# Twelve output tiles take x*Dskip from GpSimd instead of TensorE

## The chip, the cores and the metric

The kernel runs on one core of a Trainium2 chip. The metric is the device time of one execution in microseconds (us), as the median of several runs. Beside the runs there is one profiled execution, from which all views of the profile come. The engines are TensorE (PE, with its weight loads PEld), VectorE (DVE), ScalarE (ACT), GpSimd (POOL) and SyncE (SP, which here only issues DMAs). An ending q (SPq, ACTq, POOLq) means the queue on which an engine issues DMAs.

## The reference, cut to what matters

```python
x = A_x                                          # [1, 2048, 512] bf16
g = sigmoid((x * gate_w).sum(-1, keepdims=True))
a = _A_ref(x, ...)     # h[t] = Lam_bar * h[t-1] + x[t] @ B_bar ; y = 2 Re(h @ C^T) + x * Dskip
b = _B_ref(x, ...)     # linear attention, 32 heads of 16; the features are softmax(pq) and softmax(-pq)
return g * a + (1 - g) * b
```

The change concerns the term `x * Dskip` of `a`, which enters the output as `g * x * Dskip`.

## The kernel before

The 2048 rows of x are read as 16 tiles of 128 rows, with the columns transposed (`xT`, SP's DMA transposes, L229). Rows go to tiles by their residue modulo 8: tile `ti` holds the residue `r = ti // 2` of one half `a = ti % 2` of the sequence. So the scan over time becomes, for each residue, products with precomputed powers (steps g, h, z), and only residue 7 is scanned (L641).

The kernel is cut into **steps** with short names. Each is a Python generator; each `yield` ends a piece of it. A string `ORDER` (L24 to L53) lists the pieces of all steps in one order, and the loop at L804 runs down it. PE, DVE, ACT and SP take their instructions exactly in this order; POOL isn't among the engines whose order is fixed by hand (L154), but takes them as the program emits them. `@` behind a name gives the PSUM banks for what the piece allocates, `:D` puts a copy on DVE instead of ACT, `:A` puts a store on ACT's queue instead of SP's. An engine that waits in one piece holds up everything behind it in its own list. Tokens without an engine's work, such as END, only change which memory is in use.

The steps that matter here, by number n of the tile in output order (n = 0 to 15; `ti = order[n]`):

- **k, v, q** (L477 to L496): keys, values and queries, four matmuls of 512 columns each, and a copy out of PSUM.
- **X, N, E, S** for groups 1 to 3 of the query features, four tiles at a time (group 1 is tiles 4 to 7, group 2 is 8 to 11, group 3 is 12 to 15): X and N (L516, L524) take maximum and minimum by trees on DVE (L511) and subtract (L521, L527); E (L530) takes four exponentials on ACT (L138, a helper's line); S (L536) sums by a tree on DVE, takes logarithm and exponential on ACT, multiplies on DVE (L559) and then issues four DMA transposes (L563) on SP, which write `phT`. The names xA, nA, eA, sA stand for group 0, and lower-case x, n, e, s for the keys.
- **G** (L677): the gate g in four small pieces, the last a reciprocal on DVE (L684).
- **y** (L711): `py = h @ C`, two pieces of four matmuls (L717), and a third piece that adds x*Dskip: for each of four column blocks, `xT` times the diagonal matrix `Dd` (L722), into the same PSUM bank.
- **o** (L725): the attention's numerator and denominator from `phT` and `KVm` into `pn` (L736), a logarithm and a copy `nu` for each half, an exponential `rd` that takes in (1-g)/g, the product `on` on DVE (L744), and its transpose `oT`, by a DMA on SP (L758) or, for n = 12 to 15, on PE (L753).
- **t** (L761): `py += oT @ Wo` on PE (L765), then the tile is scaled by g on ACT (L769) or DVE (L771) as it leaves PSUM, then the store (L773).

So the last piece of a tile's PSUM sum is t's, and the scaling by g follows it:

```python
ot = pools["op"][1].tile([P, D], BF16, name="ot", bufs=14)
if sel["eng"] == "act":
    nc.scalar.mul(out=ot[:], in_=py[:], mul=G[:, ti:ti + 1])
else:
    VS(out=ot[:], in0=py[:], scalar1=G[:, ti:ti + 1], scalar2=None, op0=ALU.mult)
```

The memory of the query stage is taken at END (L696), when the pools of the key stage are given back.

Of the kernel before, what the change touches and what calls it, by code (L numbers as in the profile page):

```python
# [10 lines left out]
ALU = mybir.AluOpType  # L11
# [9 lines left out]
P = 128  # L21
# [8 lines left out]
a0@71 a0 x2 s1 x2 s1 v5 g00@4 g00 g60@0 n2 x3 s1 g20@3 g60 s1 g10@2 g10 n3 e2 g30@6 g40@5 g10 s1 a1 x3 g20 n3 a1 x3 n3  # L30
x3 g41@4 n3 C3 e2 e2 e2 x3 g30 g40 g30 k15@0 k15 n3 e3 s2 x4 s2 x4 g01@2 g01 e3 e3 s2 g50@3 g11@5 g50 s2 s2 s2 n4 x4
n4 Q3 n4 s2 g50 g21@6 e3 s3 v8@0 g31@2 g11 Q2 g11 n4 g70@3 Q1 s3 C7 g21 g70 v9@5 g70 g70 z0 z0 g31 g31 Q0 w1@6 C0 a2
a2 a2 w0@3 s3 z0 v11@2 v9 g61@5 g41 R4 z0 w1 v8 z0 z0 g61 s3 w2@4 s3 s3 a2 x4 z0 z0 g51@6 g51 x4 w2 C2 s3 w3@0 g51 v11
n4 R5 w3 g71@5 g71 g71 g71 z1 z1 g02@4 g02 g42@6 a3 a3 z0 z0 g42 w0 e4 e4 z1 z1 z1 g62@2 g12@0 q1@5 C1 h50@4 C5 J1 e4
# [10 lines left out]
S1 y1 E2 E2 E2 E2 y9@6 G N3 y5 y5 y3@4 y2 X3 X3 N3 t1 G t1 N3 S1 N3 S2 y9 y9 S2 S2 S1 S1 S2 y3 y3 t3 y0 t0 t0 t2 t2
y6@7 X3 t2:A o4@2 o4 o4@5 o4 o4 y6 y6 t3 X3 o4 X3 o4 S2 S2 t3 o5@1 o5 o5@2 o5 o5 y13@5 y13 o5 N3 o6@4 S2 o6 o6@1 o6 o6
y12@2 o5 y7@4 y7 y12 o6 o6 t4 y7 S2 S2 t4:D S2 E3 E3 E3 E3 S2 o7@1 o7 t5 t5 S3 o7@0 o7 S3 o7 t6 S3 o7 S2 o7 y8@1 o8@3
t6 o8 o8@0 o8 o8 S3 S3 y12 t0:A y11@7 o8 o8 o9@3 o9:D o9@0 o9:D S3 y8 y8 o9 o9 S3 S3 o9 o10@3 y11 o10 o10@0 y11 o10
o10 S3 y14@3 S3 y14 t7 t7:D t8 y14 t8 y15@0 o11@4 S3 o11 o11@1 t9 o12@4 o11:D o11 S3 o10 o10 o12 o12@1 o12 o12 t9:D
# [19 lines left out]
def kernel(  # L69
# [26 lines left out]
    NR = 8  # L96
# [614 lines left out]
    def st_y(n):  # L711
# [49 lines left out]
    def st_t(n):  # L761
# [5 lines left out]
        ot = pools["op"][1].tile([P, D], BF16, name="ot", bufs=14)  # L767
        if sel["eng"] == "act":
            nc.scalar.mul(out=ot[:], in_=py[:], mul=G[:, ti:ti + 1])  # L769
        else:  # L770
# [8 lines left out]
          "M": st_M(), "D": st_D(), "L": st_L(), "G": st_G(), "Y": st_Y(), "END": st_END(), "NR": st_N(0), "NI": st_N(1), "O": st_O()}  # L779
# [35 lines left out]
    for key in ("op", "fq", "eq", "sq"):  # L815
        pools[key][0].__exit__(None, None, None)
# [31 lines left out]
```

## Time and profile before

| | us |
|---|---|
| three runs: median (lowest to highest) | 155.84 (155.54 to 156.19) |
| profiled execution, first to last instruction | 153.2 |
| PE busy in it | 146.2 |
| DVE busy in it | 132.4 |
| ACT busy in it | 129.2 |
| POOL busy in it | 15.8 |

The profiled execution's own time is its span, 153.2 us; the runs' time is taken around the whole execution and also holds what lies before the first and after the last instruction. A busy PE is not PE at its peak: matmuls are pipelined, and their ends are modelled. In the groups of instructions a line of the view reads: line, engine, operation, out<-in with shapes, count | busy us, mean ns of one | idle time of the engine before them and who ended it. In the timeline a line reads: start us, length us, engine, line, operation. The columns of the other views are told where they are shown. The mean granted clock of PE is 0.995 over the span.

### The profile page before, as it was taken

Reading aid. Unit: us, or ns where it says so; the run is one execution under the profiler, and the core shown is the slowest. Engines: PE = TensorE matmul, PEld = TensorE weight load, DVE = VectorE, ACT = ScalarE, POOL = GpSimd, SP = SyncE. Lnnn points to the kernel's source line nnn. Section 1 sums busy time; section 2 is a strip of 40 time slices with the busy share of each in tenths; the row PEclk is TensorE's granted clock in tenths of the full one; section 3 lists DMA queues with packets and bytes.
Section 4 is the critical chain, followed back from the end, with each engine's and each line's share of the span. In section 5 each row is a group of like instructions: output and inputs, shape, how many; then the busy total and the mean of one; then the engine's idle time right before and its main releaser. Section 6 shows DMA issues by size and latency. Waiting matters only on the chain.

```text
span 153.2 us, 3361 instructions
## 1 busy us (share of the span) xinstructions
PE 146.2 (95%) x1236; PEld 95.0 (62%) x1254; DVE 132.4 (86%) x303; ACT 129.2 (84%) x279; POOL 15.8 (10%) x43
## 2 busy tenths in 40 slices
PE   7899999999999999999999999999999999999990
PEld 7644434788878985869867656555554455555540
DVE  3799999999999999999999999999999958717520
ACT  3489998999998999999998999699498998627562
POOL 8239980000000000000000000000000000000000
PEclk9999999999999999999999999999999999999997
DMA  4875995534445699930000007711278859969842
GB/s 116 164 218 97 223 178 112 103 75 103 103 107 78 129 230 178 166 115 4 0 0 4 0 0 169 74 37 34 42 98 147 176 122 189 162 129 206 247 143 103
DMA packets 50848, 17.55 MB, mean 115 GB/s; under 512 B 44176, under 2 KB 50832, under 8 KB 50832
## 3 DMA queue, kind: packets, MB, share of 16 engines
q1 hardware_dynamic: 48976, 15.75, 53.8%
q10 hardware_dynamic: 1696, 1.57, 3.2%
q8 instruction: 10, 0.16, 0.5%
q0 software_dynamic: 160, 0.01, 0.2%
q14 instruction: 6, 0.05, 0.1%
HBM read 2.64 MB, written 2.10 MB: 31 GB/s over the span
## 4 chain that ended last, share of the span: by engine, by line
PE 78%; SPq 10%; DMA 7%; issue 1%; ACT 1%
PE pgq L601 18%; PE py L717 16%; PE pq L475 9%; PE py L765 8%; SPq L229 8%; PE pv L475 4%; PE ph L668 4%; PE pk L475 4%; DMA xT<-in_A_x_dram 4%; PE kvacc L578 3%; DMA phT<-EEq 3%; PE pn L736 3%; PE pgq L606 2%; PE py L722 2%; PE pgq L608 2%; SPq L284 1%
## 5 line engine op out<-in xcount | busy, mean ns | idle before, releaser
L601 PE MATMUL pgq<-xT,BT 128*128 128x256 bf16 x256 | 31.5, 272 | 0.0
L475 PEld LDWEIGHTS <-xT 128*128 128x128 bf16 x192 | 18.2, 98 | 18.3 <-DMA xT<-in_A_x_dram 0.7
L601 PEld LDWEIGHTS <-BT 128*128 128x128 bf16 x256 | 24.6, 98 | 4.1
L138 ACT ACTIVATE EEk<-EEk 128x1024 bf16<-128x1024 bf16 x20 | 20.4, 1080 | 0.0
L119 ACT CAST uv<-pgq 128x512 bf16<-128x512 f32 x28 | 15.9, 605 | 0.5 <-PE pgq L601 0.4
L475 PE MATMUL pv<-Wv,xT 128*128 128x512 bf16 x59 | 15.5, 379 | 0.3
L475 PE MATMUL pq<-Wq,xT 128*128 128x512 bf16 x60 | 15.4, 379 | 0.2
L765 PE MATMUL py<-Wo,oT 128*128 128x512 bf16 x62 | 15.3, 379 | 0.1
L475 PE MATMUL pk<-Wk,xT 128*128 128x512 bf16 x62 | 14.7, 379 | 0.3 <-DMA xT<-in_A_x_dram 0.2
L138 ACT ACTIVATE EEq<-EEq 128x1024 bf16<-128x1024 bf16 x12 | 11.7, 1042 | 0.3 <-DVE EEq L527 0.3
L769 ACT ACTIVATE ot<-py,G 128x512 bf16<-128x512 f32 x12 | 7.9, 686 | 4.5 <-PE py L765 4.3
L138 ACT ACTIVATE ld<-pn 128x16 f32<-128x16 f32 x32 | 6.1, 191 | 5.7 <-PE pn L736 4.6
L590 ACT ACTIVATE phT<-X,dgB 128x512 bf16<-128x512 bf16 x16 | 10.7, 725 | 0.0
L119 ACT CAST nu<-pn 128x256 bf16<-128x256 f32 x27 | 9.9, 380 | 0.0
L119 ACT CAST vx<-pv 128x512 bf16<-128x512 f32 x16 | 9.1, 604 | 0.4 <-PE pv L475 0.4
L548 DVE TENSOR_TENSOR EEk<-EEk,rck 128x4096 bf16<-128x4096 bf16 (+1 forms) x5 | 9.3, 1858 | 0.0
L744 DVE TENSOR_TENSOR on<-nu,rd 128x512 bf16<-128x512 bf16 x16 | 6.7, 421 | 2.8 <-ACT rd L138 1.6
L765 PEld LDWEIGHTS <-oT 128*128 128x128 bf16 x64 | 5.7, 97 | 5.3 <-DMA oT<-on 0.5
L119 ACT CAST Xq<-pq 128x512 bf16<-128x512 f32 x16 | 8.9, 608 | 0.0
L119 ACT CAST Xq<-pk 128x512 bf16<-128x512 f32 x15 | 8.6, 598 | 0.4 <-PE pk L475 0.4
L736 PEld LDWEIGHTS <-phT 128*128 128x128 bf16 x128 | 6.2, 97 | 3.8 <-DMA phT<-EEq 1.4
L511 DVE TENSOR_TENSOR smk<-smk 128x512 bf16<-128x512 bf16 (+4 forms) x18 | 8.1, 448 | 0.1
(178 smaller groups left out, 321.2 us busy)
## 6 DMA issues: line engine op xcount, KB each, us to landing
X<-HM SPq DMA_DIRECT2D x8, 256.0 KB, 4.5
out_dram<-ot ACTq DMA_DIRECT2D x8, 128.0 KB, 2.5
out_dram<-ot SPq DMA_DIRECT2D x8, 128.0 KB, 2.2
C2r<-in_B_wqkv_dram ACTq DMA_DIRECT2D x2, 256.0 KB, 3.8
Wv<-in_B_wqkv_dram SPq DMA_DIRECT2D x1, 512.0 KB, 4.0
Bn<-in_A_B_re_dram SPq DMA_DIRECT2D x1, 512.0 KB, 5.7
Bn<-in_A_B_im_dram SPq DMA_DIRECT2D x1, 512.0 KB, 6.8
Wo<-in_B_wo_dram SPq DMA_DIRECT2D x1, 512.0 KB, 4.3
```

The lines of the kernel that those rows point to most:

```text
L119: nc.scalar.copy(out=out_ap, in_=in_ap)
L138: ins = nc.scalar.activation(**kw)
L229: nc.sync.dma_start_transpose(out=xT[:, :, ti * P:(ti + 1) * P], in_=x_res[ti // 2, ti % 2])
L475: MM(out=pt[:], lhsT=xT[:, kt, ti * P:(ti + 1) * P], rhs=W[:, kt, :], start=(kt == 0), stop=(kt == KT - 1))
L511: VT(out=dst, in0=cur[:, :, :, 0:n, :], in1=cur[:, :, :, n:2 * n, :], op=op)
L548: VT(out=E5, in0=E5, in1=rc.to_broadcast([P, L, 2 * NB, Dh, 4]), op=ALU.mult)
L590: nc.scalar.mul(out=t_, in_=x_, mul=c_)
L601: MM(out=pg[:, h, :], lhsT=BT[:, kt, 2 * j + h, :], rhs=xT[:, kt, r * NC:(r + 1) * NC], start=(h == 0 and kt == 0), stop=(r % 2 == 0 and k ...
L717: MM(out=py[:], lhsT=hs(r, t, slice(a * P, (a + 1) * P)), rhs=C2B[t], start=(t == 0), stop=False)
L736: MM(out=pn[:, 4 * m:4 * m + 4, :].rearrange("p h e -> p (h e)"), lhsT=ph[:, 4 * hf + m, :], rhs=KVm[:, 4 * hf + m, :], start=(m == 0), st ...
L765: MM(out=py[:], lhsT=oT[:, g, :], rhs=Wo[:, g, :], start=False, stop=(g == HG - 1))
L769: nc.scalar.mul(out=ot[:], in_=py[:], mul=G[:, ti:ti + 1])
```

## The change

For the twelve tiles n = 4 to 15 the third piece of y goes away, and x*Dskip is computed by GpSimd from the plain (not transposed) rows of x. One new step, XL, loads these rows once more, all residues but 7, on POOL's queue, with Dskip repeated over the partitions. Twelve new steps Z4 to Z15 each multiply the rows of one tile by Dskip, in place, and scale the product by g into a tile `gx` of four buffers. The t step of these tiles then computes `py * g + gx` in one DVE instruction, whatever engine the list names. The tile `ot` gets 8 buffers instead of 14. The list ORDER is drawn up anew from its first token to its last.

```diff
+SKIP_PE = (0, 1, 2, 3)
+OTB = 8
@@ st_END
+        enter("xp", name="xrows", bufs=1)
@@
+    def st_XL():
+        xp = pools["xp"][1]
+        xr = xp.tile([P, 2, NR - 1, D], BF16, name="xr")
+        dr = xp.tile([P, D], BF16, name="dr")
+        live["xr"], live["dr"] = xr, dr
+        rows = x2.rearrange("(a c r) d -> c a r d", r=NR, c=P)
+        for a in range(2):
+            nc.gpsimd.dma_start(out=xr[:, a], in_=rows[:, a, 0:NR - 1])
+        nc.gpsimd.dma_start(out=dr[:], in_=A_Dskip.unsqueeze(0).to_broadcast([P, D]))
+        yield
+
+    def st_Z(n):
+        ti = order[n]
+        gx = pools["xp"][1].tile([P, D], F32, name="gx", bufs=4)
+        live["gx", n] = gx
+        xs = live["xr"][:, ti % 2, ti // 2, :]
+        GT(out=xs, in0=xs, in1=live["dr"][:], op=ALU.mult)
+        nc.gpsimd.tensor_scalar(out=gx[:], in0=xs, scalar1=G[:, ti:ti + 1], scalar2=None, op0=ALU.mult)
+        yield
@@ st_y
+        if n not in SKIP_PE:
+            return
         for kt in range(KT):
@@ st_t
-        ot = pools["op"][1].tile([P, D], BF16, name="ot", bufs=14)
-        if sel["eng"] == "act":
+        ot = pools["op"][1].tile([P, D], BF16, name="ot", bufs=OTB)
+        if n not in SKIP_PE:
+            nc.vector.scalar_tensor_tensor(out=ot[:], in0=py[:], scalar=G[:, ti:ti + 1], in1=live["gx", n][:], op0=ALU.mult, op1=ALU.add)
+        elif sel["eng"] == "act":
```

Of the list, the first lines and the part behind END (the old list's twelve third pieces of y are gone in the new one, and XL and Z4 to Z15 are new):

```diff
-NR F:28 NI B W1@0 W0@1 W0 W2@2 W1:D W3@3 W3 f1@4 W2:D f0@5 f2@6 f0 f1:D l10 V@0 F:4 V P f3@1 f3 f2:D F:4 P P k1@2 k1
+F:28 W0@1 W1@2 W2@3 B W3@4 W0:D W1:D f0@1 W3 l10 f1@2 W2:D f0:D F:4 f2@3 f3@4 f3:D f1 f2 V@1 V U U P NI NR F:4 U k0@2
...
+h43 h20 q8@4 h53 h40 sA q10 c7 c7 q9@6 h63@3 q8 sA h63 h23@4 h23 sA END G q11@0 h02 o0@1 h01 o0 o1@2 N1 q12@3 q11 X1
+y3@1 N1 o2@0 o0@4 N1 q9 X1 X1 o1 o0 X1 o1@2 o2 o0 X1 y5@6 N1 y0@4 o3@0 o1 q12 N1 y1@2 y2@3 y3 o1 X2 E1 E1 N2 o2@7 E1
+N2 o0 E1 XL y0 o2 X2 X2 y2 o1 o2 y5 o3 o0 X2 q15@5 N2 N2 o3@7 X2 y2 S1 o3 y1 y3 S1 S1 q15 S1 o1 o3 o2 o3 y9@5 S1 S1 N2
+y4@7 y0 S1 y1 S1 y6@0 o2 o3 G E2 t1 S1 E2 X3 y4 E2 X3 N3 t2 t0 t3 y9 E2 X3 G t2 X3 N3 S1 t1 N3 o4@2 S1 t0 N3 S2 Z4 S2
+S2 o4:D o4@4 S2 y6 o4 o4 o5@4 S1 t3 Z5 o5 o4 o5@2 y12@3 o6@4 y13@1 X3 o5 o5 S2 o5 t1 o6 S2 o6@2 y13 o7@4 S2 N3 o4 o6
+y7@2 t4 o6 o5 o6 y7 E3 Z6 t5 t3 E3 S2 o7:D o7@4 o6 t4:D E3 y8@7 t6 t5 S2 y12 E3 o7 o7 S2 t2:A o8@4 S3 S2 o8 t6 Z7 o8@6
+y11@0 o8 Z9 o8 Z12 o9@4 o9 Z8 S2 o9@6 o7 S3 S3 S3 o8 S3 y8 o9:D o7 o9 y14@4 S3 t0:A y14 o10@6 S3 t7 o9 o8 o10 y11 S3
+o9 S3 t6:A o10@6 t8 t7:D o10 t8 o11@6 y15@2 o11 o11@6 o11:D S3 S3 o10 t9 o12@6 o10 o12 t9:D S3 o11 Z11 Z15 o12@7 o12:D
+y15 o11 o12 o13@5 o12 y10@6 o12@7 o13 o13@5 o13:D y10 Z10 o14@5 o10 o12 o14:D o14@7 o13 t12 o14:D o11 o15@5 o13 t4:A
+t5 o15 o15@7 t12 t9 t10 o14 o13@3 o15:D o15 o15 t11 Z13 o15@7 t7:A o13 o15 o14 t8 o14@3 o14 t10:D t12:A t11 t13 t13
+t15 t15 t15 Z14 t14 t13 t10 t11:A t14 t14:A
```

Elsewhere in the new list SP issues NI and NR (the loads of B's imaginary and real part, L284) behind l10 instead of at the head, v0's copy out of PSUM is on DVE (`v0:D`), and o4's first copy too (`o4:D`).

More of the change, by code (lines that the diff above doesn't have):

```diff
@@ L30 @@
[L30 to L34, printed above, removed]
@@ L45 @@
[L45 to L49, printed above, removed]
@@ L50 @@
-o11 y15 o13@4 o13:D o13@6 t6:A o13 o13 o11 o12 y10@1 o14@4 y15 o14:D o12@6 t9 o12:D t7:A t1 y10 y10 o13 o15@4 o15
-o15@6 t4:A t5 o15 o15 t8 o15 t12 t12 t12:A t10 o14@4 o14 o14 t10:D o13@6 t11 o15@2 o15 t10 o13:D t11 t11:A y13 t13 o14
-o14@1 t15 t15 t15 o14:D t14 t13 t13 t14 t14:A
+F:28 W0@1 W1@2 W2@3 B W3@4 W0:D W1:D f0@1 W3 l10 f1@2 W2:D f0:D F:4 f2@3 f3@4 f3:D f1 f2 V@1 V U U P NI NR F:4 U k0@2
+l11 P P2 P2 l12 P2 P2 U P2 k0 P4 V2@1 P4 P P2 k1@4 k2@2 V2 k3@1 P3 P4 i0 v3@3 i2 l9 k1 i0 l13 i0 i1 i2 i0:D P3 i0 i2
@@ new lines @@
+i2:D i2 i1 l8 k4@4 i1 k5@0 v0@5 k6@6 x0 i3 R0 x0 x0 i3 k7@7 n0 x0 n0 R1 x0 v3 v7@3 k3 n0 gw k2 n0 n0 n1 l15 v5@2 i3
+l14 R5 i1 i3 x1 i1 v2@1 x1 n1 x1 i3 k4 k7:D k6 R3 v4@6 x1 C4 x1 k5 n1 n1 L v0:D n1 M e0 v6@5 e0 n2 n2 v4 C2 x2 k11@0
+k10@7 x2 s0 v1@6 s0 s0 e1 s0 C1 k13@4 x2 k11 s0 v2 e1 n2 k10 k12@1 s0 k8@0 k9@7 D s0 v5 s1 g20@2 s1 s1 v1 v7 k9 v6 s1
+R2 a0@73 a0 x2 k8 k13 k12 Q1 n2 x2 g60@5 Q3 s1 g60 n2 g00@4 k14@1 x3 g70@5 g00 s1 s1 g10@4 e2 n3 k15@0 x3 g20 x3 O k14
+a1 n3 a1 x3 g10 g40@1 e2 n3 e2 g10 e2 g30@2 n3 x3 g30 n3 g40 k15 s2 g01@4 g50@0 Q0 e3 n4 g01 C7 g30 e3 g31@1 g50 s2 s2
@@ L792 @@
     for n in range(NTI):
-        st.update({f"k{n}": st_k(n), f"v{n}": st_v(n), f"q{n}": st_q(n), f"y{n}": st_y(n), f"o{n}": st_o(n), f"t{n}": st_t(n)})
+        st.update({f"k{n}": st_k(n), f"v{n}": st_v(n), f"q{n}": st_q(n), f"y{n}": st_y(n), f"o{n}": st_o(n), f"t{n}": st_t(n), f"Z{n}": st_Z(n)})
     for n, (t0_, L_) in enumerate(KG):
@@ L814 @@
         next(st[tok])
-    for key in ("op", "fq", "eq", "sq"):
+    for key in ("xp", "op", "fq", "eq", "sq"):
         pools[key][0].__exit__(None, None, None)
```

26 lines of the change are left out of this document (11 added, 15 removed).

## The prediction

> **What bounds the kernel now.** I read the page's busy times and its chain first, then the stretches of time, then who waits for whom.
>
> ```profile
> span 153.2 us, 3361 instructions
> PE 146.2 (95%) x1236; PEld 95.0 (62%) x1254; DVE 132.4 (86%) x303; ACT 129.2 (84%) x279; POOL 15.8 (10%) x43
> PE 78%; SPq 10%; DMA 7%; issue 1%; ACT 1%
> ```
>
> PE is on 78% of the chain that ends last, but VectorE (DVE) and ScalarE (ACT) are close behind it, so I need to see where DVE is full. The columns below are length, then busy time of PE, PEld, DVE, ACT and POOL, then the granted clock, the DMA share and GB/s.
>
> ```profile
> 100.00:105.00 5.00, 5.00 (x31) 2.40 (x30) 5.00 (x12) 4.74 (x15) 0.00 (x0) 1.00 0.12 27
> 105.00:110.00 5.00, 4.95 (x39) 2.79 (x39) 4.97 (x12) 3.49 (x9) 0.00 (x0) 1.00 0.27 52
> 115.00:120.00 5.00, 5.00 (x42) 2.58 (x40) 4.67 (x12) 4.42 (x13) 0.00 (x0) 1.00 0.84 157
> 120.00:125.00 5.00, 4.76 (x29) 2.16 (x29) 3.92 (x6) 4.67 (x13) 0.00 (x0) 1.00 0.71 153
> 130.00:135.00 5.00, 4.95 (x44) 2.69 (x44) 2.94 (x6) 2.55 (x11) 0.00 (x0) 1.00 0.88 144
> ...
> PEld L736 <- DMA phT<-EEq: 1.4, 3, 0.7
> PEld L475 <- DMA xT<-in_A_x_dram: 0.7, 1, 0.7
> ```
>
> Two things are to be seen. DVE is full until about 120 us and has room only after that; POOL does nothing at all. And where PE waits late in the run, it waits for phT, the transposed query features: these come from DVE, by the steps X, N, E, S and four DMA transposes for each group of four tiles. So the end is set by PE and by DVE's feature chain together, and time off PE is a gain only if DVE keeps up.
>
> **The change, part by part.** *Removed from PE:* the third piece of y for twelve tiles.
>
> ```profile
> 114.80 0.22 PE py L722 x4
> ...
> L769 ACT ACTIVATE ot<-py,G 128x512 bf16<-128x512 f32 x12 | 7.9, 686 | 4.5 <-PE py L765 4.3
> L771 DVE TENSOR_SCALAR ot<-py,G 128x512 bf16<-128x512 f32 x4 | 3.0, 750 | 4.2 <-PE py L765 4.1
> L672 DVE TENSOR_TENSOR Bn<-ph,uv 128x512 bf16<-128x512 f32 x8 | 5.4, 684 | 0.0
> L121 DVE CAST nu<-pn 128x256 bf16<-128x256 f32 x5 | 2.0, 423 | 2.6 <-ACT ld L138 2.6
> ...
> 19.18 0.68 DVE L121 CAST Xq<-pk 128x512 bf16<-128x512 f32 x1
> ```
>
> That is 12 x 0.22 = 2.64 us of PE, all on the path while PE is full; ahead of step o8 the old list has nine of these pieces and the new one four, so 1.1 us of it falls there. *Moved to DVE:* the twelve last scalings. They read py from PSUM and gx from SBUF; no row has this very form, L672 (684 ns) and L771 (750 ns) lie on both sides, and I take 0.7 us, 8.4 us for twelve. The old list had 12 scalings on ACT and 4 on DVE, the new one 4 and 12. They fall behind 123 us, where DVE has room. The new list also puts v0's copy (0.68) and half of o4's (0.42) on DVE, ahead of or inside group 2's feature chain: 1.1 us where DVE is full. The other moved copies of the list lie where DVE has slack.
>
> *Added on POOL:* per tile one product of two bf16 tensors of 128x512 and one scaling of 128x512. The trace has no such product. These rows are nearest, the rows of DVE beside them included:
>
> ```profile
> L384 POOL TENSOR_TENSOR ssm_par<-dl,vec 128x16 f32<-128x16 f32 x1 | 0.3, 265 | 0.0
> ...
> 18.57 0.69 DVE L527 TENSOR_TENSOR EEk<-mnk,Xq 128x1024 bf16<-128x1024 bf16 x1
> 18.57 0.75 POOL L404 TENSOR_TENSOR dl<-ssm_par 128x4 f32<-128x4 f32 x1
> 19.28 0.20 POOL L405 TENSOR_TENSOR dl<-ssm_par 128x4 f32<-128x4 f32 x1
> 21.56 0.70 DVE L511 TENSOR_TENSOR smk<-EEk 128x1024 bf16<-128x1024 bf16 x1
> 21.80 0.97 POOL L320 TENSOR_SCALAR_AFFINE_SELECT Dd<-vec 128x512 bf16<-128x512 f32 x1
> 22.19 0.86 DVE L511 TENSOR_TENSOR mnk<-mnk 128x512 bf16<-128x512 bf16 x1
> 22.97 0.41 DVE L511 TENSOR_TENSOR smk<-smk 128x512 bf16<-128x512 bf16 x1
> ```
>
> They say more than a duration. POOL's L404 takes 0.75 us where its twin L405 takes 0.20: it ends just behind a DVE instruction that began with it. The other way round, DVE's mnk at 22.19 takes 0.86 us where an equal shape takes 0.41, and it overlaps L320, which ends at 22.77. So **POOL and DVE shut each other out**, one instruction at a time, where DVE reads two tensors from SBUF. L320 itself seems to have waited for smk until 22.26; what is left, 0.51 us, is POOL's price for 512 elements with one input. For the product the lower end is the same 0.5; the upper end is the slope from L405 to L384, 65 ns for 12 elements, or 0.27 + 496 x 5.4 ns = 2.9 us. I take 1.0, two inputs at the price of one each, since L320 is the only row with this number of elements. So a tile costs 1.5 us and twelve cost 18 us.
>
> The Trainium skill, "SBUF — State Buffer", section "SBUF: two separate sides", states this as an exclusive lock: whichever of a GpSimd instruction and a DVE instruction with two SBUF inputs starts first keeps the shared port, and "the other fully blocks". The rows at 18.57 and 22.19 agree with it, though some rows of POOL that begin beside DVE are too short to tell. The same skill's "GPSIMD Engine Reference", section "Performance versus the Vector engine", gives about 2.6 cycles per element at 1.2 GHz for two inputs; an estimate from that page is 1.1 us for 512, and the sum would be 0.3 us higher by it.
>
> *What a POOL instruction costs DVE:* between nothing (POOL waits, as L404 did) and 0.45 of 0.51 us (mnk). Nearly every DVE instruction of the feature chain reads two SBUF tensors, so I lean to mnk's row, but L405 ran its 0.20 beside the copy from PSUM at 19.18 and neither was longer for it, so what POOL runs there, or in a pause of DVE, costs nothing: I take **0.6 of POOL's time**.
>
> *The load XL* moves 1.97 MB (1.84 of x, 0.13 of Dskip) on POOL's queue. Its memory lay under the key features, so it waits for the last of these transposes:
>
> ```profile
> 90.82 7.83 SPq L563 DMA_TRANSPOSE phT<-EEk  x4
> ...
> L251 POOL DMA_DIRECT2D vec_m<-in_A_Dskip_dram x1 | 0.5, 518 | 0.0
> ```
>
> It can start at about 101 us (98.65 and some 2.5 us to land), at 0.5 us an issue, when the DMA engines are 12 to 27% busy. At the 215 GB/s that 153 GB/s at a share of 0.71 make, it takes 9 us and is there by 110. G, which Z4's scaling needs, is ready at about 115. So the load is hidden; if it came ten us later it would lie among the phT and oT transposes and push them by up to a microsecond or two.
>
> *The step list.* Early on PE stays full: SP issues the two B loads behind l10 instead of ahead of it, and the first k steps are ordered to suit; the 0.7 us wait for xT is what can move there, either way. The ot tile has 8 buffers instead of 14: t11's scaling now waits for t4's store, which ACT issues at about the time of t12's scaling; two scalings, a copy and two products of o lie between on DVE, some 2.5 us by their rows, and a store on that queue lands in 2.5 (below), so 0 to 0.5 us, of which I take nothing.
>
> **The sum**, along the feature chains of groups 2 and 3:
>
> ```profile
> 114.97 0.25 DVE L684 RECIPROCAL G<-G 128x16 f32<-128x16 f32 x1
> ...
> 121.24 1.22 DVE L527 TENSOR_TENSOR EEq<-mnq,Xq 128x2048 bf16<-128x2048 bf16 x1
> 122.49 3.90 ACT L138 ACTIVATE EEq<-EEq 128x1024 bf16<-128x1024 bf16 x4
> 122.94 1.22 DVE L559 TENSOR_TENSOR EEq<-EEq,rhoq 128x2048 bf16<-128x2048 bf16 x1
> 124.61 5.39 SPq L563 DMA_TRANSPOSE phT<-EEq  x4
> 126.58 1.22 DVE L511 TENSOR_TENSOR smq<-EEq 128x2048 bf16<-128x2048 bf16 x1
> 128.57 0.51 PEld L736 LDWEIGHTS <-phT 128*128 128x128 bf16 x8
> 132.00 1.23 DVE L559 TENSOR_TENSOR EEq<-EEq,rhoq 128x2048 bf16<-128x2048 bf16 x1
> 138.25 0.63 PEld L736 LDWEIGHTS <-phT 128*128 128x128 bf16 x8
> ...
> DMA to landing us min/median/max: 3.2/3.3/4.4
> ...
> 148.34 1.84 ACT L769 ACTIVATE ot<-py,G 128x512 bf16<-128x512 f32 x3 [1.00 <-PE py L765]
> out_dram<-ot ACTq DMA_DIRECT2D x8, 128.0 KB, 2.5
> ```
>
> Four buffers of gx let POOL run four tiles ahead: between G and the end of S2 it has four products and four scalings, 6.0 us, 0.6 of which is 3.6 us for DVE. S2 ends at 124.16 today; then at 124.16 + 1.1 + 3.6 = 128.9, its first transpose lands 3.3 us later at 132.2, and o8 begins there instead of at 128.57: **3.6 us late**, with PE waiting, since its list is fixed. N3 ends 1.1 + 3.2 us late (seven of the eight POOL instructions lie ahead of it), so ACT's four exponentials and then S3 begin at 126.58 + 4.3 = 130.9. S3's stretch lasts 6.65 us today (126.58 to 133.23); it gains 0.3 (t6's scaling, less one copy) and three products and scalings of POOL, 4.5 x 0.6 = 2.7, and gives back about 0.6 in which DVE now idles: S3 ends at 139.95, phT lands at 143.25, and o12 begins 5.0 us late. Behind o12 PE saves three pieces, 0.66. The last scaling costs 0.75 instead of 0.69. In all 5.0 - 0.66 + 0.06 = **+4.4 us: a span of 157.6**. The runs' median of 155.84 stands 2.64 above the profiled span, which I carry over: **160.2 us**.
>
> **The rivals.** *A, hidden:* POOL gets in only where DVE leaves the port. Then PE saves 2.64, but S2 ends 1.1 late while PE comes 1.1 early, against a slack today of 0.67 (landing at 127.91, o8 at 128.57) and 0.45 (SP issues 0.45 behind S2), so 1.1 comes back: 1.5 to 2.6 us faster, 153.2 to 154.3, say 153.8: **faster**. For it: L404, and DVE's room behind 120. Against it: mnk. The share scales the lock's 5.9 us (3.2 and 2.7), so it decides below about 0.07 instead of 0.6. *B, POOL is the bound:* with 2.9 us a product the tile costs 3.4, twelve 41 us from 111 on; with some 9 us behind DVE, the last scaling comes at 161, and the span ends 3.8 us later: 164.8, or 167.4 on the runs' scale. For it: the slope. Against it: L320. *C, a wash:* gain and lock cancel at a share of about 0.15 (9.8 x 0.15 = 1.5). *D, the change does not do what it says:* XL lands behind 124 and t4 stands at the head of DVE's queue with S3 behind it. The margin is 14 us, so it is nearly nothing; it would look like B.
>
> **Chances.** The forecast (157 to 164 us) 0.6, A 0.2, C 0.08, B with D 0.12. A measurement of this kernel can tell about 0.5% from no change, 0.8 us. Faster 0.2, the same 0.08, slower 0.72. The range reaches from the slow half of A, 153.7, to B's price, 167.5; the forecast's own range is 157 to 164.
>
> **What would show it.** Right: POOL busy near 34 us in all, its products near 1 us and longer beside DVE; DVE's two-input rows from 115 us on longer than the 1.22 and 0.42 of today; PE's wait for phT grown from 1.4 us to 5 or more, at o8 and o12. Wrong: these rows unchanged and PE full (A); DVE standing at the scalings for gx, with POOL full (B); or a loss that lies ahead of 100 us, in the reordered list, which I put at nothing.

## The result and the profile after

The changed kernel takes 174.62 us (median of 4 runs, 173.78 to 175.49) beside 155.69 us of the kernel before in the same session (155.41 to 156.19): a ratio of 1.122, 95% interval 1.117 to 1.126. It is slower, as forecast, but by 18.9 us instead of 4.4, and outside the range. Where the runs of a kernel fall into a faster and a slower group (e1, e5, e6, e7 and e13 below), a ratio is that of the faster group, while the time given is the median of all its runs.

The page of the changed kernel's profile, first the busy times, then the granted clock in 40 slices, then the chain that ended last:

```profile
span 173.8 us, 3302 instructions
...
PE 152.4 (88%) x1188; PEld 95.0 (55%) x1206; DVE 155.4 (89%) x314; ACT 125.2 (72%) x268; POOL 53.5 (31%) x70
...
PEclk9999969999999999999999999999696569999998
...
DVE 38%; SPq 33%; PE 15%; DMA 8%; issue 4%; ACT 1%; DVEq 0%; ACTq 0%
```

PE has gone from 78% of the chain to 15; VectorE and SP's queue have taken its place. POOL is busy 53.5 us instead of 15.8, and PE's clock, full nearly throughout before, drops to 5 and 6 tenths in four of the slices from 122 us on (and in one at 22 us), each time behind gaps of PE. The groups of its two new lines and of the new scaling (busy, mean ns, idle time in front):

```profile
L725 POOL TENSOR_SCALAR gx<-xr,G 128x512 f32<-128x512 bf16 x12 | 21.5, 1797 | 15.2 <-DVE ot L794 15.2
...
L724 POOL TENSOR_TENSOR xr<-xr,dr 128x512 bf16<-128x512 bf16 x12 | 17.3, 1475 | 6.2 <-DMA dr<-in_A_Dskip_dram 6.2
...
L794 DVE SCALAR_TENSOR_TENSOR ot<-py,G,gx 128x512 bf16<-128x512 f32 x12 | 8.9, 748 | 3.8 <-PE py L790 3.6
```

POOL's timeline shows their order:

```profile
115.02 17.29 POOL L724 TENSOR_TENSOR xr<-xr,dr 128x512 bf16<-128x512 bf16 x12 [6.23 <-DMA dr<-in_A_Dskip_dram]
132.30 7.99 POOL L725 TENSOR_SCALAR gx<-xr,G 128x512 f32<-128x512 bf16 x4
145.28 1.56 POOL L725 TENSOR_SCALAR gx<-xr,G 128x512 f32<-128x512 bf16 x1 [4.99 <-DVE ot L794]
```

All twelve products run in one row, 17.29 us long, as soon as the rows have landed; then four scalings into the four gx buffers; then the other eight, most of them waiting for a buffer. This isn't the order in which the Z steps emit them: each step emits its product and then its scaling, so the order that I gave for POOL ahead of the prediction (as the program emits) was wrong. POOL is the engine whose order the kernel leaves open (L154); where its order was made, the runs don't show. VectorE's timeline beside that burst:

```profile
117.67 2.66 DVE L769 TENSOR_TENSOR on<-nu,rd 128x512 bf16<-128x512 bf16 x2
120.25 1.23 DVE L555 TENSOR_TENSOR dlq<-lgq 128x128 f32<-128x128 f32 x1
121.40 2.17 DVE L529 TENSOR_TENSOR EEq<-mnq,Xq 128x2048 bf16<-128x2048 bf16 x1
123.49 2.17 DVE L561 TENSOR_TENSOR EEq<-EEq,rhoq 128x2048 bf16<-128x2048 bf16 x1
125.58 1.12 DVE L684 TENSOR_SCALAR G<-G 128x16 f32<-128x16 f32 x1
```

Before, L529's form took 1.22 us, and dlq 0.28. VectorE is "busy" all the time, but of the 13 instructions that it begins between 115.05 and 131.3 us, long or short, all but two (a 128x1024 maximum and G's reciprocal) first stand behind one of POOL's products. The stretches of time (length, then PE, PEld, DVE, ACT, POOL, then clock, DMA share, GB/s) say what that does to PE:

```profile
115.00:120.00 5.00, 4.11 (x25) 1.92 (x23) 4.93 (x5) 0.42 (x1) 4.98 (x4) 1.00 0.08 15
120.00:125.00 5.00, 3.48 (x9) 1.33 (x10) 5.00 (x4) 1.71 (x3) 5.00 (x5) 0.67 0.27 52
125.00:130.00 5.00, 1.83 (x8) 0.68 (x7) 4.96 (x5) 2.50 (x3) 5.00 (x4) 0.99 0.63 118
130.00:135.00 5.00, 1.93 (x12) 1.00 (x12) 4.90 (x9) 3.05 (x8) 5.00 (x4) 0.69 0.59 123
135.00:140.00 5.00, 3.85 (x20) 1.82 (x20) 4.96 (x9) 2.46 (x10) 5.00 (x3) 0.50 0.13 26
```

In each 5 us up to 130 VectorE has 4 or 5 instructions beside POOL's 4 or 5 (12 before at 105 to 110). PE works 11.4 of the 20 us up to 135, and what it waits for stands in the waits (total, times, longest):

```profile
PE pn L761 <- ACT ot L796: 6.2, 2, 6.0
...
ACT ot L796 <- DVE G L686: 4.1, 1, 4.1
...
PEld L761 <- DMA phT<-EEq: 3.9, 2, 2.7
...
PE py L790 <- DMA oT<-on: 3.5, 2, 2.4
...
PE pn L761 <- DMA phT<-EEq: 0.7, 1, 0.7
```

ACT's first scalings wait for G, whose reciprocal VectorE begins at 131.2 instead of 115.0 us, and PE waits for the PSUM banks that these scalings free.

### The profile page after: what moved, and what is told of

It reads as the page before. It is cut to its first block, busy times and chain, and to the rows that moved or that the text cites. A ratio compares the mean times of both kernels' runs of the same rounds, so it can differ in the third digit from the quotient of the medians.

```text
span 173.8 us, 3302 instructions
## 1 busy us (share of the span) xinstructions
PE 152.4 (88%) x1188; PEld 95.0 (55%) x1206; DVE 155.4 (89%) x314; ACT 125.2 (72%) x268; POOL 53.5 (31%) x70
## 4 chain that ended last, share of the span: by engine, by line
DVE 38%; SPq 33%; PE 15%; DMA 8%; issue 4%; ACT 1%; DVEq 0%; ACTq 0%
SPq L231 12%; PE py L740 7%; SPq L298 6%; SPq L290 6%; PE py L790 5%; SPq L303 4%; DVE mxq L513 4%; DMA X<-HM 4%; DVE smq L513 3%; DVE mnq L513 3%; DMA phT<-EEq 3%; SPq L294 3%; DVE Bn L674 3%; DVE on L769 2%; DVE HM L674 2%
## 5 line engine op out<-in xcount | busy, mean ns | idle before, releaser
L715 POOL DMA_DIRECT2D xr<-in_A_x_dram x2 | 1.2, 600 | 86.7 <-DMA phT<-EEk 86.7
L725 POOL TENSOR_SCALAR gx<-xr,G 128x512 f32<-128x512 bf16 x12 | 21.5, 1797 | 15.2 <-DVE ot L794 15.2
L790 PE MATMUL py<-Wo,oT 128*128 128x512 bf16 x62 | 17.2, 412 | 3.6 <-DMA oT<-on 3.5
L724 POOL TENSOR_TENSOR xr<-xr,dr 128x512 bf16<-128x512 bf16 x12 | 17.3, 1475 | 6.2 <-DMA dr<-in_A_Dskip_dram 6.2
L477 PE MATMUL pk<-Wk,xT 128*128 128x512 bf16 x62 | 16.4, 405 | 1.1 <-DMA xT<-in_A_x_dram 1.0
L477 PE MATMUL pv<-Wv,xT 128*128 128x512 bf16 x59 | 15.2, 379 | 1.8 <-DVE vx L123 1.6
L477 PE MATMUL pq<-Wq,xT 128*128 128x512 bf16 x60 | 15.5, 378 | 0.5 <-DVE HM L674 0.3
L761 PEld LDWEIGHTS <-phT 128*128 128x128 bf16 x128 | 7.7, 104 | 14.9 <-issue 7.1
L761 PE MATMUL pn<-KVm,phT 128*128 128x68 bf16 x128 | 8.9, 204 | 7.9 <-ACT ot L796 6.2
L592 ACT ACTIVATE phT<-X,dgB 128x512 bf16<-128x512 bf16 x16 | 11.7, 740 | 0.9 <-DMA X<-HM 0.8
L794 DVE SCALAR_TENSOR_TENSOR ot<-py,G,gx 128x512 bf16<-128x512 f32 x12 | 8.9, 748 | 3.8 <-PE py L790 3.6
L769 DVE TENSOR_TENSOR on<-nu,rd 128x512 bf16<-128x512 bf16 x16 | 8.5, 544 | 1.2 <-ACT rd L140 1.1
```

What stands on the lines that cost most here:

```text
L477: MM(out=pt[:], lhsT=xT[:, kt, ti * P:(ti + 1) * P], rhs=W[:, kt, :], start=(kt == 0), stop=(kt == KT - 1))
L724: GT(out=xs, in0=xs, in1=live["dr"][:], op=ALU.mult)
L725: nc.gpsimd.tensor_scalar(out=gx[:], in0=xs, scalar1=G[:, ti:ti + 1], scalar2=None, op0=ALU.mult)
L761: MM(out=pn[:, 4 * m:4 * m + 4, :].rearrange("p h e -> p (h e)"), lhsT=ph[:, 4 * hf + m, :], rhs=KVm[:, 4 * hf + m, :], start=(m == 0), st ...
L769: VT(out=on[:].rearrange("p g h (a b) -> p (g h) a b", b=4), in0=nu[:].rearrange("p c h (a b) -> p (c h) a b", b=4), in1=rd[:].unsqueeze(2 ...
L790: MM(out=py[:], lhsT=oT[:, g, :], rhs=Wo[:, g, :], start=False, stop=(g == HG - 1))
```

## The experiments

My theory: GpSimd's arithmetic costs VectorE, and by it PE, because the two shut each other out, and most of it because it comes in one burst. The rivals: the loads and the scaling's second input cost, not the arithmetic; or the new list costs by itself. The last of these turned out to hold a part. In e3, e4, e10, e14 and e16 to e18 x*Dskip of twelve tiles is left out or replaced by zeros.

### GpSimd's arithmetic and its burst

**e3**: the changed kernel with the loads, but gx a constant zero.

```diff
-        GT(out=xs, in0=xs, in1=live["dr"][:], op=ALU.mult)
-        nc.gpsimd.tensor_scalar(out=gx[:], in0=xs, scalar1=G[:, ti:ti + 1], ...)
```

> The changed kernel with XL's loads, but without the twelve products and twelve scalings on GpSimd: gx is one tile of zeros, so x*Dskip is left out for twelve tiles. Theory 1: only the list's early cost stays, less 2.6 us of TensorE, and the clock stays up: 157 to 161. Theory 3: 170 or more. If the load XL itself were a cost (its 1.97 MB run at a DMA share of 1.0 from 110 to 115), this run would stay 2 us or more above the list alone less 2.6.

161.99 us, ratio 1.041 (1.034 to 1.048), a shade over the upper end of the first answer. The arithmetic is worth 174.6 - 162.0 = **12.6 us**; the other **6.3** are there without it, and with PE's 2.64 us saved.

**e4**: each of the 24 GpSimd instructions replaced by a memset of the tile that it wrote.

> The changed kernel with each GpSimd product and scaling replaced by a memset of the same tile, so GpSimd writes as much and reads nothing from SBUF (x*Dskip is left out for twelve tiles). If the exclusion is between VectorE's two-input instructions and GpSimd instructions that read: within 1 us of the run without GpSimd arithmetic, VectorE's rows at their 1.22 and 0.42. If any GpSimd instruction takes the port: each memset delays one VectorE instruction by its own length, some 0.4 us (by the 205 ns of a 128x128 memset), and the time lies 4 to 8 us above that run.

161.71 us, ratio 1.039 (1.031 to 1.046): as e3. POOL's timeline, then VectorE's, in e4:

```profile
115.28 3.79 POOL L724 MEMSET xr<- 128x512 bf16 x8
```

```profile
116.36 1.22 DVE L529 TENSOR_TENSOR EEq<-mnq,Xq 128x2048 bf16<-128x2048 bf16 x1
117.50 1.22 DVE L561 TENSOR_TENSOR EEq<-EEq,rhoq 128x2048 bf16<-128x2048 bf16 x1
118.64 0.46 DVE L684 TENSOR_SCALAR G<-G 128x16 f32<-128x16 f32 x1
```

The same instruction that took 2.17 us beside a product takes its 1.22 beside eight memsets. So for VectorE's instructions with two inputs it is not that POOL works, nor its writes; it is that it reads SBUF. The Trainium skill, "SBUF — State Buffer", section "SBUF: two separate sides", limits the lock against a two-input VectorE instruction to a GpSimd instruction that reads SBUF; e4 agrees with it. One row goes the other way: G's addition, with one input, took 0.46 us here instead of 0.17 and ended with the last of the eight memsets (119.1), so that instruction seems to wait even for a POOL instruction that only writes.

**e5**: the product written into the gx tile, so that it needs a free buffer, and scaled there.

```diff
-        GT(out=xs, in0=xs, in1=live["dr"][:], op=ALU.mult)
-        nc.gpsimd.tensor_scalar(out=gx[:], in0=xs, ...)
+        GT(out=gx[:], in0=xs, in1=live["dr"][:], op=ALU.mult)
+        nc.gpsimd.tensor_scalar(out=gx[:], in0=gx[:], ...)
```

> The changed kernel, with the product written into gx instead of over the rows of x, and scaled there. So a product needs a free gx buffer and can't run more than four tiles ahead: GpSimd does as much, but not in one burst of twelve products. Theory 1a (the burst is what costs: it takes every second turn of the port while VectorE is full): the burst is 4 products and 4 scalings, 4 x 1.3 + 4 x 1.6 = 11.6 us instead of 17.3 + 8.0 = 25.3 between 115 and 140, so 5 to 9 us come back: 165 to 170. Theory 1b (the sum of GpSimd's time is what costs, wherever it lies): 173 to 176.

167.95 us, ratio 1.079 (1.073 to 1.086), the first answer: 6.7 us come back, with the same arithmetic. POOL's timeline in e5:

```profile
115.36 5.03 POOL L724 TENSOR_TENSOR gx<-xr,dr 128x512 f32<-128x512 bf16 x4 [6.24 <-DMA dr<-in_A_Dskip_dram]
125.43 7.88 POOL L725 TENSOR_SCALAR gx<-gx,G 128x512 f32<-128x512 f32 x4 [5.05 <-DVE G L686]
137.01 1.16 POOL L724 TENSOR_TENSOR gx<-xr,dr 128x512 f32<-128x512 bf16 x1 [3.71 <-DVE ot L794]
```

Now POOL runs four tiles ahead and no further, which is the number that the prediction had assumed, though these four products still run ahead of G. The burst is 6.7 us of the loss, the rest of the arithmetic 6.0.

**e2**: the whole change on the old list (its twelve third pieces of y taken out, XL behind the second N2, the Z steps behind G and behind the scalings).

> The old list, only without the twelve third pieces of y, with XL where group 1's features begin and the Z steps behind G; everything else as in the changed kernel. Theory 1: the GpSimd burst costs about 12 us net of the 2.6 us that TensorE saves, 165 to 169; the first sum of group 1 is back at 107. Theory 2: all of the loss, 172 to 175. Theory 3 (the list is what costs, GpSimd is mostly hidden): 154 to 158.

169.13 us, ratio 1.085 (1.078 to 1.092), at the upper end of the first answer, with the first sum of S1 back at 107.1: GpSimd's work costs with the old list too.

**e13**: e2 with e5's edit.

> The old list with GpSimd's work for twelve tiles (as e2, 169.1 us), but the product written into the gx tile, so that GpSimd runs at most four tiles ahead (as e5). If burst and list are separate losses that add up: e2 less the 6.6 us that e5 gained, 161.5 to 164.5 us. If the old list had hidden part of the burst already: 165 to 169.

165.75 us, ratio 1.068 (1.063 to 1.073), the second answer: 3.4 us less than e2 and not 6.7. Burst and list do not simply add up.

### Where GpSimd's work lies

**e8**: the old list, GpSimd for the last four tiles alone (`SKIP_PE` is 0 to 11), the load as in e2.

> The old list with GpSimd computing x*Dskip for four tiles only (12 to 15), the load XL unchanged. TensorE saves 0.9 us. Theory 1: the four products (4 x 1.4 = 5.8 us) still fall where VectorE is full, from 111 us on, the four scalings behind G; each takes about its length from VectorE's feature chain, so 3 to 6 us worse than before: 158 to 161, a third or so of the 13.5 us that twelve tiles cost on this list. If what costs isn't GpSimd's work but having twelve scalings with a second operand on VectorE: 155 or less.

160.15 us, ratio 1.030 (1.025 to 1.035): four tiles cost 4.7 us. POOL's timeline in e8 shows them at 110 to 128 us, mostly in VectorE's full stretch:

```profile
109.98 6.58 POOL L724 TENSOR_TENSOR xr<-xr,dr 128x512 bf16<-128x512 bf16 x4 [6.25 <-DMA dr<-in_A_Dskip_dram]
119.28 9.13 POOL L725 TENSOR_SCALAR gx<-xr,G 128x512 f32<-128x512 bf16 x4 [2.72 <-DVE mnq L513]
```

**e15**: e8 with GpSimd's work tied to the end of that stretch. Ahead of the first product, one column of S3's last result (`em`) less itself, so zero, is added to Dskip's first column.

```diff
+        em = live["EE", "G3"][:, 3, 7, 1, 63:64]
+        GT(out=z0[:], in0=em, in1=em, op=ALU.subtract)
+        GT(out=live["dr"][:, 0:1], in0=live["dr"][:, 0:1], in1=z0[:], op=ALU.add)
```

> The kernel of e8 (old list, GpSimd for tiles 12 to 15, load early, 160.2 us), with two one-column GpSimd instructions ahead of the first product that read the last result of S3, so that GpSimd's work begins only behind VectorE's feature chain (about 133 us). If GpSimd costs what it takes from VectorE while that is full: 155 to 157 us. If GpSimd's own time is then the bound (four products and four scalings, 11.7 us, so the last at about 145 and the scaling of the last tiles behind it): 157 to 160.

157.01 us, ratio 1.010 (1.007 to 1.014), where the two answers meet: the price falls from 4.7 to 1.6 us. The second answer asks that the last scalings wait for POOL; none of VectorE's waits in e15 is for gx. POOL's and VectorE's timelines in e15:

```profile
134.08 2.26 POOL L729 TENSOR_TENSOR xr<-xr,dr 128x512 bf16<-128x512 bf16 x2
136.33 3.12 POOL L730 TENSOR_SCALAR gx<-xr,G 128x512 f32<-128x512 bf16 x2
```

```profile
139.94 0.92 DVE L774 TENSOR_TENSOR on<-nu,rd 128x512 bf16<-128x512 bf16 x1
```

Alone a product takes 1.15 us and a scaling 1.56. The lock is still there (0.92 where 0.42 is usual), but VectorE has room, so little of it reaches the end.

**e12**: the same aim by another way: the rows loaded on SP's queue behind the last transpose of S2.

> The old list; GpSimd computes x*Dskip for the last four tiles (12 to 15) as in the change, but the rows are loaded on SP's queue behind the last transpose of S2, so that the products cannot start ahead of about 129 us, where VectorE has room. If what costs is GpSimd's arithmetic beside VectorE's feature chain: between 155 and 157 us, against the 160.2 of the same four tiles with the early load. If the cost is in the scalings with a second input or in waiting for GpSimd at the end: 158 to 161.

159.9 us, ratio 1.027 (1.024 to 1.031): the second answer by its time, but not by its reason. A stretch and a wait of PE in e12:

```profile
135.00:140.00 5.00, 2.68 (x14) 1.13 (x13) 0.75 (x1) 0.48 (x1) 2.66 (x3) 1.00 0.89 124
```

```profile
PE py L790 <- DMA oT<-on: 2.3, 1, 2.3
```

PE, VectorE and ScalarE stand while the transposes of oT are late; the five loads stood ahead of them on SP's queue (130.3 to 132.9 us), and the DMA engines are 89% busy. The load spoils the test, which is why e15 was made.

**e11**: four tiles (10, 13, 14, 15) without GpSimd: VectorE computes gx in one instruction behind S3. (In e11 and e12 one copy of o14 also goes from VectorE to ScalarE.)

```diff
-        GT(out=xs, ...)
-        nc.gpsimd.tensor_scalar(out=gx[:], ...)
+        nc.vector.scalar_tensor_tensor(out=gx[:], in0=xs, scalar=G[:, ti:ti + 1], in1=live["dr"][:], op0=ALU.mult, op1=ALU.mult)
```

> The old list; x*Dskip of four tiles (10, 13, 14, 15) computed by VectorE itself in one instruction each, (x times G) times Dskip, behind the last step of S3, from rows loaded by GpSimd's queue behind the second N2 step; GpSimd computes nothing. PE does 0.88 us less, behind 128 us. If the loss of the change comes from GpSimd's work beside VectorE and from the list, this one is 0.2 to 0.9 us faster than before: 154.8 to 155.5. If the scaling's second input itself costs time, or VectorE's four extra instructions (0.75 us each) delay the last tiles: 156 to 157.

155.76 us beside 155.80, ratio 1.001 (0.998 to 1.004): no difference, and between the two answers. Loads and scalings with a second input, without GpSimd's arithmetic, are no large term for these four tiles. But 0.88 us less for PE, behind 128 us, bring nothing visible either: with VectorE's four more instructions the sum is nil, and the two are not taken apart. The full load is in e3, which does not lie the 2 us above e1 (next section) less PE's 2.64 that its expectation names as the sign of a cost. No version beat the kernel before.

### The list

**e1**: the new list alone: Dskip's piece back on PE for all tiles, no loads, no GpSimd, plain scalings.

> The new list with x*Dskip back on TensorE for all sixteen tiles (the four matmuls follow the second piece of y), no load XL, no GpSimd work; the twelve scalings stay on VectorE. Theory 1 (the lock and the list each have a share): in the changed kernel group 1's first sum already began at 113.1 us, 6.1 later than before, ahead of any GpSimd arithmetic, so the list alone costs about 5 to 7 us: a median of 161 to 163. Theory 2 (only GpSimd's work costs anything; what was late at 113 would have been caught up): 155 to 157.

165.44 us (163.28 to 166.19), ratio 1.054 (1.042 to 1.065), more than either theory asked; PE has its 2.64 us of work back here. Most of the loss is there by the first sum of S1: it begins on VectorE at 113.2 us in e1 instead of 106.9, and at 113.1 in the changed kernel, ahead of the first product of GpSimd. Early on, PE in the changed kernel's timeline:

```profile
21.30 1.04 PE L477 MATMUL pv<-Wv,xT 128*128 128x512 bf16 x4 [1.57 <-DVE vx L123]
23.32 3.25 PE L477 MATMUL pk<-Wk,xT 128*128 128x512 bf16 x8 [0.99 <-DMA xT<-in_A_x_dram]
...
30.73 1.04 PE L603 MATMUL pgq<-xT,BT 128*128 128x256 bf16 x8
```

PE waits for v0's copy on VectorE and for xT, and the first pgq comes 1.8 us later than before (28.93).

**e6** and **e7** (both on e1) take back one suspect each: `v0:D` becomes `v0`; NR and NI go to the head of the list.

> The new list alone (e1_list_alone), with v0's copy back on ScalarE. In the changed kernel TensorE stood 1.57 us at 21.3 us for a bank that this copy on VectorE gave back late. If that wait is what the list loses early: about 2 us better than e1_list_alone (163 or less). If another wait of the same moment takes its place (the x tile that comes 1.0 us late just behind it): the same within 1 us.

> The new list alone, with the two loads of B issued at the head of their group on SP as before, ahead of l10. If SP's order of these loads costs TensorE its wait for x: 1 to 2 us better than e1_list_alone. If the order only moves the wait (x tiles then come later, since the loads are ahead of them): the same or worse.

165.41 and 166.03 us, but the runs scatter by up to 4.7 us: e6 has one run of 161.67 and three from 165.05 on, e7 one of 163.44 and three from 165.96 on. So neither shows a gain of 2 us, and neither excludes it. In e6's profile PE waits 2.5 us for xT instead. The following build on e3, which is steadier.

Comparing VectorE's instructions up to the first sum of S1, I found their number and kinds almost equal (245 before, 248 in e3), but not their spacing. VectorE's timeline before, and in the changed kernel:

```profile
28.07 0.69 DVE L511 TENSOR_TENSOR smk<-EEk 128x1024 bf16<-128x1024 bf16 x1
28.67 0.29 DVE L511 TENSOR_TENSOR mxk<-mxk 128x256 bf16<-128x256 bf16 x1
28.87 0.42 DVE L511 TENSOR_TENSOR smk<-smk 128x512 bf16<-128x512 bf16 x1
```

```profile
30.03 0.69 DVE L513 TENSOR_TENSOR smk<-EEk 128x1024 bf16<-128x1024 bf16 x1
30.75 1.08 DVE L513 TENSOR_TENSOR smk<-smk 128x512 bf16<-128x512 bf16 x3
```

Before, mxk begins 0.09 us ahead of the end of smk, since it reads another tile. In the changed kernel the next smk, which reads the last one's result, begins 0.03 behind it. Over the whole stretch independent neighbours lie at -0.08, dependent ones at +0.03 or +0.04: 0.115 us each. By the two lists, 6 neighbours are dependent before and 41 after; in the traces 39 instructions of the stretch begin 0.01 to 0.06 us behind the one before them, and 74 after, which is 35 more as well.

**e9**: the kernel before, with twelve VectorE instructions one place forward.

```diff
-n0 x0 n0 x0
+n0 n0 x0 x0
...
-a0 x2 s1 x2 s1 v5
+a0 x2 x2 s1 s1 v5
```

> The kernel before with twelve VectorE instructions of its list moved forward by one place each, so that 30 instructions ahead of the first sum of S1 follow directly on the one whose result they read, instead of 6; nothing else differs. Theory 1 (the reordered list costs time because a VectorE instruction that reads the result of the one just before it starts 0.03 us behind that one's end, instead of 0.08 us ahead of it): 24 x 0.115 = 2.8 us, so 157.6 to 158.6 us, and the first sum of S1 at 109.4 to 109.9 in place of 106.9. Theory 2 (the list costs time by PE's early waits and its order of loads alone): 155.2 to 156.3 us.

158.05 us, ratio 1.016 (1.013 to 1.020): 2.25 us for 24 more dependent neighbours. The first sum of S1 comes at 110.1, 3.2 us late and 0.2 later than I had allowed. Moving twelve instructions by one place, then, costs this kernel 1.6%; by the table below, 2.1 of the 3.2 us are overlap that the neighbours lose, and 1.1 are more idle time.

**e10** does the reverse on e3, from 41 to 16.

> The kernel of e3 (the new list, without GpSimd's products and scalings: x*Dskip of twelve tiles is left out) with twenty VectorE instructions moved by one or two places, so that 16 instead of 41 follow directly on the one whose result they read. Theory 1 (dependent neighbours on VectorE): 25 x 0.115 = 2.9 us less than the 162.0 of e3, so 158.6 to 160 us, and the first sum of S1 at 110.0 to 110.6 instead of about 113. Theory 2 (PE's early waits and the order of loads): 161 to 162.5 us, the first sum where it was.

161.34 us, ratio 1.039 (1.034 to 1.045): 0.65 us instead of 2.9, so the first answer fails, although VectorE's busy time up to the first sum falls by 1.8 and that sum comes 0.9 us earlier. **e14** gives e3 the first 150 tokens of the old list, **e16** does both.

> The kernel of e3 (new list, GpSimd computing nothing, x*Dskip of twelve tiles left out, 162.0 us), with the first 150 tokens of the old list at its head and the new list's order behind them; 36 dependent neighbours on VectorE instead of 41. If the head (PE's stalls at 20 to 25 us, its order of loads) costs what the neighbours do not explain: 159.5 to 160.7 us, first sum of S1 at 110.3 to 111.3 instead of 112.4. If the neighbours are nearly all of it: 161.2 to 162.2.

> The kernel of e14 with eighteen VectorE instructions moved by one or two places, so that 13 instead of 36 follow directly on the one whose result they read. If head and neighbours together are the list's loss: 23 x 0.115 = 2.6 us less than e14, and with PE's 2.64 us saved the time comes to 156.5 to 158.5. If what the neighbours give back turns into a wait, as in e10: within 0.8 us of e14.

161.24 us, ratio 1.038 (1.033 to 1.042), and 160.84, ratio 1.035 (1.030 to 1.039): again 0.75 and 1.15 us of the 6.3. Differences of this size from e3 (161.15 to 162.31) lie within the scatter of the runs. e14 lies at the edge of the second answer, with the first sum at 112.9 and not earlier than in e3; e16 gives the second. Why so little comes back stands in the stretch from 60 to 70 us of e16:

```profile
60.00:70.00 10.00, 8.93 (x75) 7.13 (x73) 8.85 (x18) 8.78 (x16) 0.00 (x0) 1.00 0.65 127
```

VectorE has 1.15 us of idle time there, and e3 only 0.22. Most of it is a wait for ACT's phT, which waits for the X loads of SP's queue (e16's waits):

```profile
ACT phT L592 <- DMA X<-HM: 1.1, 1, 1.1
...
DVE C2i L596 <- ACT phT L592: 0.8, 1, 0.8
```

These loads begin at 54.6 in e3, 54.2 in e16 and 55.0 in the changed kernel, but at 50.8 before. SP's timelines of the kernel before and of the changed one:

```profile
50.83 5.64 SPq L301 DMA_DIRECT2D X<-HM  x6
56.52 2.75 SPq L288 DMA_TRANSPOSE BT<-Bn  x1
```

```profile
53.51 1.27 SPq L290 DMA_TRANSPOSE BT<-Bn  x1
55.01 9.01 SPq L303 DMA_DIRECT2D X<-HM  x8
```

The new list issues two BT transposes and the Wo load ahead of X; the old one issues them behind its first six X loads. **e18** moves these three behind X in e3, **e17** in e16 (`R7`, `R6` and `O` behind the last `J2`).

> The kernel of e3 (162.0 us) with the same three moved behind the last X load, and nothing else. VectorE has hardly a gap at 60 to 70 us there (9.78 of 10 busy), since its dependent neighbours keep it full: if the two bounds stand in for each other as I think, 161.2 to 162.3 us. If SP's queue alone is the list's loss: 158.5 to 160.5.

> The kernel of e16 (old head, neighbours apart, GpSimd computing nothing, x*Dskip of twelve tiles left out, 160.8 us) with two BT transposes and the Wo load moved behind the last X load on SP's queue, so that the X loads begin about 3.2 us earlier. If the X loads are what VectorE then waits for: the 1.2 us of idle time at 60 to 70 us go, first sum of S1 at 109.4 to 110.4 instead of 111.4, 158.5 to 159.9 us. If not: 160.4 to 161.4.

161.18 us, ratio 1.039 (1.032 to 1.046), at the edge of its first answer, and **159.23** us, ratio 1.023 (1.017 to 1.029), its first. Alone the move brings 0.8 us, within the scatter, and on top of the other two 1.6; all three together bring 2.8, with every run of e17 below every run of e3. The mechanism is smaller than I expected, though: X begins at 52.8 in e17, 1.4 us earlier than in e16 and not 3.2, and the idle time at 60 to 70 us falls to 0.71 instead of going. The chains that ended last, of e3, of e18 and of e17:

```profile
DVE 37%; SPq 36%; DMA 11%; PE 8%; issue 4%; ACT 2%; DVEq 0%; ACTq 0%
```

```profile
DVE 62%; PE 15%; DMA 9%; ACT 6%; issue 5%; DVEq 0%; ACTq 0%
```

```profile
SPq 37%; PE 23%; DVE 17%; DMA 12%; ACT 5%; issue 4%; ACTq 0%; DVEq 0%
```

SP's queue is gone from e18's chain, and VectorE has taken its place, at the same time of the whole: two bounds within a microsecond of each other. In e17 SP's queue is back on the chain with 37%. VectorE's side of it up to the first sum of S1, in us (the busy time is that of the stretch, the sum that of count times mean of all groups, so what neighbours overlap is sum less busy time):

| kernel | begins at | sum | busy | overlap | idle | time |
|---|---|---|---|---|---|---|
| before | 106.9 | 119.1 | 102.5 | 16.6 | 4.5 | 155.7 |
| e9 | 110.1 | 119.0 | 104.5 | 14.5 | 5.6 | 158.1 |
| e3 | 112.4 | 120.0 | 106.6 | 13.4 | 5.9 | 162.0 |
| e10 | 111.5 | 119.9 | 104.7 | 15.1 | 6.8 | 161.3 |
| e16 | 111.4 | 119.1 | 103.9 | 15.2 | 7.5 | 160.8 |
| e17 | 110.5 | 119.2 | 103.8 | 15.5 | 6.8 | 159.2 |

e3's 5.5 us at this point are 3.2 of lost overlap, 0.9 of more work (v0's copy among it) and 1.4 of idle time.

## Why the prediction was wrong in size

On the new list the loss divides into 6.3 us of the list, net of what PE saves (e3), 6.7 of the burst (from e5 to the changed kernel) and 6.0 of the rest of GpSimd's arithmetic (from e3 to e5).

**The step that failed first**: "Four buffers of gx let POOL run four tiles ahead: between G and the end of S2 it has four products and four scalings". The product is written in place into the loaded rows; it needs neither gx nor G, so no operand held it. Twelve products ran ahead, before G and into the very chain that makes G. I read the Z steps' place in the list as POOL's order, though the diff shows that only the scaling touches gx. e5, which limits POOL to four tiles ahead, gives 6.7 us back.

**The second**: "The step list. Early on PE stays full: ... the 0.7 us wait for xT is what can move there, either way", taken at nothing but for 1.1 us of two copies. The list costs 6.3 us, even with 2.64 us less for PE. I asked only what the list does to PE, and not how VectorE's instructions follow on one another, or how late SP's X loads come, although I had written that VectorE was full up to 120. The prediction named this, a loss ahead of 100 us, as what would show it wrong.

**Mis-sized terms.** Scaling on POOL: 0.5 us taken, 1.56 alone (the shortest of the twelve; 1.80 in the mean). L320, the row that I went by, is another operation. Product: 1.0 taken, 1.15 the shortest, 1.48 in the mean. The estimate of 1.1 us worked out from the Trainium skill's "GPSIMD Engine Reference" ("Performance versus the Vector engine") agrees with the shortest. A tile costs 3.3 us instead of 1.5, POOL's waits for the port included. This is nearly rival B's 3.4 by chance (B took it from a product of 2.9), and POOL was not the bound at the end as B says: it waited 15.2 us for VectorE to free gx. VectorE's scaling: 0.7 taken, 0.75 measured.

**What was right.** The direction. The lock: VectorE's two-input rows lengthen, and these only beside a POOL instruction that reads (e4). The share of 0.6: from the first sum of S1 to G's reciprocal VectorE took 18.1 us in the changed kernel (113.08 to 131.22) and 7.9 in e3 (112.44 to 120.30); the 10.3 us between them, over POOL's 16.2 in that time, are 0.63. What remains of the arithmetic once POOL is held to four tiles (e5), 6.0 us, is close to the forecast's 5.9, partly by luck, since the durations were too short and four products still ran ahead of G. The smaller ot tile: no wait on a store appears among VectorE's. The load: it landed at 115 instead of 110, as it waited for the key features' transposes and was issued at 107.0 instead of 101 (SP's part of them ended at 103.1, 4.4 us later than before); it was still ahead of t4, so D is out. A asked for a share below 0.07, and C for 0.15; both are out.

**Signs that misled.** I expected POOL to be busy for 34 us; it was for 53.5. I expected the wait for phT to grow from 1.4 us, a row of PEld, to 5 or more. PEld's row reads 3.9, PE's own wait for phT is 0.7, and the largest is PE's 6.2 for ACT's scalings behind G: G stood in VectorE's delayed queue ahead of the rest, and so it became the wait. Nothing of PE's 2.64 us is left in the changed kernel's time, though on the new list the work is worth something: e1's runs, with it back on PE, lie 1.3 us and more above e3's median.

**Open.** e17 still lies 3.5 us above the kernel before, though PE has 2.64 us less to do, so more than half of the list's 6.3 us is unexplained. 13 dependent neighbours remain in it, and 2.3 us more idle time of VectorE, and SP's queue has 37% of its chain; I have not taken these apart. Why e13 gained 3.4 us and e5 6.7 is not settled either, nor what set the order of POOL's instructions.

## What to carry to other kernels

Before an engine off the path is given work, ask what its instruction depends on by its operands, not where it stands in the program: here the products, which needed nothing that was late, ran at once, in a burst, beside what was then the bound. Work of GpSimd that reads SBUF was paid for by VectorE at about 0.6 of its time where VectorE was full, nearly all with two-input instructions, and far less where it had room (four tiles: 4.7 us, or 1.6 behind its chain). And where a full engine is drawn up anew, count the neighbours that depend on each other, and look at every queue: bounds close to one another give little back when only one is mended (0.65, 0.75 and 0.8 us alone, all within the scatter, and 2.8 together).

## What the runs showed of the hardware

- Beside the burst GpSimd and VectorE take turns, one instruction each, so a short VectorE instruction pays as much as a long one: G's 128x16 addition took 1.12 us instead of 0.17, dlq 1.23 instead of 0.28, and L529's 128x2048 row 2.17 instead of 1.22, each 0.95 longer.
- A memset of GpSimd (0.52 us) lengthens no two-input VectorE instruction in e4's burst (115 to 119 us), but G's one-input addition took 0.46 us beside it instead of 0.17.
- GpSimd's scaling of one tensor by a column (1.56 us for 512 elements) is slower than its product of two tensors (1.15), from bf16 and, in e5, from f32 alike.
- A VectorE instruction that reads its neighbour's result starts 0.115 us later against that neighbour's end (0.03 behind it) than one that does not (0.08 ahead of it).
- PE's granted clock falls behind its gaps: 0.50 in 135 to 140 us, behind 10 us in which PE was busy for 3.8. Four matmuls of 512 columns then took 1.90 us instead of 1.03. The Trainium skill, "TensorE: Matmul & The Clock Gate", section "Part 1: The HAM clock gate", says that the array runs at half rate after an idle window of about 3.4 us. The 6.0 us wait ahead of 132.9 and the 0.50 agree with it. But the clock also fell to 0.67 in 120 to 125 us, behind a wait of only 2.4 us (119.2 to 121.5), so here a shorter gap was enough.
